# Attention and a gated MLP on one core: chunks 0 and 1 walk the weight tiles together, each unit's v comes in one transfer, and six attention units form the prologue

## The chip, the cores and the metric

The kernel runs on one core of one Trainium2 chip. The time is the device time of one execution in microseconds. The core's engines run side by side, each through its own instructions in a fixed order: TensorE (PE in the rows; its weight loads are PEld), VectorE (DVE), ScalarE (ACT), GpSimd (POOL) and SyncE (SP), whose queue issues all the transfers here.

## The reference

The first part is attention over 4 batches of 8 heads, 576 positions and 64 columns. Its output is the sum of a coarse attention over means of four positions, repeated four times, and a local one over the positions closer than 4. The second part is a two-layer MLP with 512 inputs, 2048 inner columns and 512 outputs.

```
q_d = q.reshape(B, H, Sd, 4, D).mean(axis=3)            # k_d, v_d alike
out_up = np.repeat(sm_attn(q_d, k_d, v_d), 4, axis=2)
mask = np.abs(pos[:, None] - pos[None, :]) < 4
out_local = softmax(np.where(mask, scale * q @ k.T, -1e9)) @ v
x = (out_up + out_local).transpose(0, 2, 1, 3).reshape(B * S, H * D)   # 2304 x 512
h = x @ w_in                                            # 2304 x 2048
g = h * np.tanh(np.log1p(np.exp(h)))
out = g @ w_out                                         # 2304 x 512
```

All of it is float32; the two weight matrices come as float64.

## The kernel before

**Attention units.** `attention(b, p, ...)` makes one unit: batch b and one pair of heads p, so 16 units of 576 columns. A unit loads its q and k (`qk`) and its v; VectorE pools q and k (L345); TensorE makes the coarse scores (`sc`, L360) and the local ones (`sl`, L390); softmax follows on VectorE and ScalarE (L363 to L405); TensorE transposes (`at`, `pt`) and multiplies with v (`pvo`, `pve`, L441 and L467); VectorE adds the two parts (L480) and splits the result into a high and a low part (L494). That is `x{p}_{c}`, in the layout that the MLP reads: x of p holds 128 of the 512 inputs, c is a chunk of 384 of the 2304 rows. A batch has 576 rows, so chunk 0 needs the four units of batch 0, and chunk 1 needs those of batches 0 and 1. v comes in three transfers: `vw`, windows of 48 positions on two groups of 48 partitions for the local part, and `vc` on 72 partitions, from which GpSimd (L415, L417) makes the pooled `vd`.

**Weights.** `load_w(f)` brings the tile of 128 inner columns f of `w_in` (`wi`) and `w_out` (`wo`) as 64-bit words into a `stg` buffer, of which there are three, and turns them into a high and a low float32 part: per half two ScalarE (L526, L535) and four VectorE instructions (L527, L529, L532, L536). There are 16 f tiles. They stay on the chip.

**Slots.** `slot(s, c, f, ...)` is one chunk with one f tile; there are 96. Twelve h matmuls (L553: four groups of three, one group for each p) fill one of two h buffers in PSUM. The gate follows: ScalarE L567, VectorE L568, ScalarE L570, L571, L573, VectorE L574, ScalarE L577, VectorE L579, which gives `g`. Then come nine acc matmuls (L590: three groups of three), which add to the chunk's three acc banks in PSUM. `SEGS` sets the walk: chunk 0 with f 0 to 4, chunk 1 with f 0 to 7, chunk 0 with f 5 to 15, chunk 1 with f 8 to 15, then chunks 2 to 5 one after the other. Where a segment ends early, ScalarE copies its three acc banks to SBUF (`parts`, L599), and the last segment of the chunk adds them (L605).

**The order.** Nothing is put in order by hand. `Plan.op` records each step with an estimated duration, its reads and writes and a priority; `Plan.order` places the steps, and each engine then runs what stands in its list, in that order. The priority of a step of slot s is about s, of its acc matmuls s + LAG - 0.5 (`LAG`: for s below 20, below 60 and above), of f tile f `WPRI[0] + WPRI[1] * f` (plus `WPRI[2]` for wo), of a unit `ATT` and `UNIT`, and of its v transfers `VOFF` more. The first `NPRO` units are the prologue: they use `SETS` buffer sets of their own beside the common set `att`, take them in turn, and share PSUM banks that the MLP's h and acc buffers take over only when the prologue is done. While TensorE has nothing to do, `fill` puts in matmuls on the identity (L686, `warm`, or into unused columns of an h bank).

Of the kernel before, what the change touches and what calls it, by code (L numbers as in the profile page):

```python
# [280 lines left out]
class Kernel:  # L281
    def __init__(self, tc, qk, vw, vc, w_in, w_out, out):
        self.tc, self.nc = tc, tc.nc
        self.qk, self.vw, self.vc = qk, vw, vc
# [256 lines left out]
    def slot(self, s, c, f, first, last, final):  # L541
        nc, pl = self.nc, self.plan
        op = pl.op
        h = pl.buf("moeps", "h", [P, 512], F32, 2, f"h{s}")
# [38 lines left out]
        if first:  # L583
            self.acc = [pl.buf("moeps", f"acc{i}", [P, 512], F32, 1, f"acc{s}_{i}") for i in range(3)]
        for i in range(3):
            a_ = self.acc[i]
# [16 lines left out]
            if (c, i) in self.part:  # L603
                part = self.part[c, i]
                op("dve", dve(512), lambda part=part, a_=a_, o=o: nc.vector.tensor_tensor(  # L605
                    out=o()[:, :512], in0=a_(), in1=part[0]()[:, c], op=ALU.add), r=[a_, part], w=[o], prio=s + 1)
            elif i % 2:
# [8 lines left out]
    def run(self, ctx):  # L616
# [44 lines left out]
        def slots(segs):  # L661
            nonlocal s
            for c, f0, f1, final in segs:
                for f in range(f0, f1):
                    self.slot(s, c, f, f == f0, f == f1 - 1, final)
                    s += 1
# [40 lines left out]
def _layout(np, q, k, v, moe_w_in, moe_w_out):  # L707
# [17 lines left out]
    return dict(qk=qk, vw=vw, vc=v2.reshape(B, H // 2, S // 8, 2, 4, 2 * D), w_in=w_in, w_out=w_out)  # L725
# [24 lines left out]
```

## Time and profile before

| | |
|---|---|
| median of 3 runs | 529.82 us (528.88 to 531.0) |
| profiled execution | 531.34 us |
| its span, first to last instruction | 529.3 us |
| mean granted TensorE clock | 0.990 |
| TensorE busy | 511.8 us (97%), 4997 matmuls |
| VectorE, ScalarE busy | 330.6 us (62%), 348.8 us (66%) |
| GpSimd busy | 39.0 us (7%) |
| moved by DMA | 43.60 MB, mean 82 GB/s |

Busy time is the time in which an engine executes; matmuls overlap one another, and so a busy TensorE need not be at its peak, and the filler matmuls count as busy too. The span lacks the 2 us around the first and the last instruction. The three runs lie 0.4% apart.

### The profile page before, as it was taken

How to read it: one execution, taken by the hardware profiler on the slowest of the kernel's cores; microseconds unless marked ns; L12 is line 12 of the kernel's file. 1: busy time of each engine (PE TensorE's matmuls, PEld its weight loads, DVE VectorE, ACT ScalarE, POOL GpSimd, SP SyncE). 2: the span in 40 equal slices, each digit the busy share in tenths (PEclk: the TensorE clock that was granted, in tenths of full speed). 3: DMA queues.
4: the chain of work that ended last, by engine and by line, in shares of the span. 5: the costliest groups of instructions: out<-in, count | busy, mean ns of one | idle time of the engine just before them, and what ended most of it. 6: DMA issues, size and time to landing. Idle time of an engine off the chain costs nothing.

```text
span 529.3 us, 11973 instructions
## 1 busy us (share of the span) xinstructions
PE 511.8 (97%) x4997; PEld 444.8 (84%) x4997; DVE 330.6 (62%) x696; ACT 348.8 (66%) x793; POOL 39.0 (7%) x53
## 2 busy tenths in 40 slices
PE   6799989999999999999999999999999999999997
PEld 4676778989999988887887888888898898989885
DVE  5599999999999353588887756524334243343333
ACT  3265867999988757475666667665656656566573
POOL 4421110000000000031211100000000000000000
PEclk9798999999999999999999999999999999999999
DMA  8764765434453010254444211100001000010001
GB/s 240 179 196 125 200 174 164 139 130 153 124 176 98 2 59 1 77 165 119 126 129 127 59 47 41 56 0 1 1 0 61 1 1 0 1 60 1 0 1 60
DMA packets 12950, 43.60 MB, mean 82 GB/s; under 512 B 1760, under 2 KB 1760, under 8 KB 12896
## 3 DMA queue, kind: packets, MB, share of 16 engines
q1 hardware_dynamic: 12896, 42.83, 27.0%
q8 instruction: 39, 0.64, 0.5%
q14 instruction: 15, 0.12, 0.1%
HBM read 38.11 MB, written 4.72 MB: 81 GB/s over the span
## 4 chain that ended last, share of the span: by engine, by line
PE 71%; DVE 6%; ACT 1%; issue 0%; DVEq 0%; ACTq 0%
PE acc L590 33%; PE h L553 32%; PE pve L467 1%; DVE x L494 1%; PE at L428 1%; PE pvo L441 1%; PE pvo L467 1%; PE sc L360 1%; PE pt L452 1%; DVE x L480 1%; PE sl L390 1%; DVE cst L365 1%; DVE cst L363 1%; DVE L_att L399 0%; DVE lst L398 0%; DVE mH L574 0%
## 5 line engine op out<-in xcount | busy, mean ns | idle before, releaser
L553 PE MATMUL h<-x,wi 128*128 128x384 f32 x1152 | 220.8, 340 | 0.7 <-DVE mH L574 0.5
L590 PE MATMUL acc<-wo,g 128*128 128x512 f32 x864 | 216.8, 396 | 0.5 <-DVE g L579 0.5
L553 PEld LDWEIGHTS h<-x,wi 128*128 128x128 f32 x1152 | 200.9, 188 | 11.4 <-DVE mH L574 3.0
L590 PEld LDWEIGHTS acc<-wo,g 128*128 128x128 f32 x864 | 160.0, 188 | 31.5 <-DVE g L579 0.9
L579 DVE SCALAR_TENSOR_TENSOR g<-mH,g 128x384 fp32r<-128x384 f32 (+1 forms) x98 | 55.5, 568 | 65.0 <-ACT g L577 64.9
L568 DVE TENSOR_SCALAR mA<-mA 128x384 f32<-128x384 f32 (+1 forms) x98 | 35.8, 366 | 89.7 <-ACT mA L567 89.5
L567 ACT ACTIVATE mA<-h 128x384 f32<-128x384 f32 (+1 forms) x98 | 47.0, 482 | 51.1 <-PE h L553 50.1
L570 ACT ACTIVATE mA<-mA 128x384 f32<-128x384 f32 (+1 forms) x98 | 50.6, 517 | 25.2 <-DVE mA L568 24.4
L577 ACT ACTIVATE g<-mH 128x384 fp32r<-128x384 f32 (+1 forms) x98 | 50.2, 515 | 22.6 <-PE acc L590 22.0
L571 ACT ACTIVATE mA<-mA,one 128x384 f32<-128x384 f32 (+1 forms) x98 | 59.3, 606 | 2.0
L574 DVE SCALAR_TENSOR_TENSOR mH<-mA,h 128x384 f32<-128x384 f32 (+1 forms) x98 | 52.9, 543 | 7.2 <-ACT mA L573 5.0
L573 ACT ACTIVATE mA<-mA 128x384 f32<-128x384 f32 (+1 forms) x98 | 50.2, 513 | 1.7
L415 POOL TENSOR_TENSOR vc<-vc 72x512 f32<-72x512 f32 x16 | 21.9, 1370 | 208.2 <-DVE cst L365 148.9
L367 ACT ACTIVATE A<-sc,cst 128x144 f32<-128x144 f32 x48 | 17.8, 375 | 17.2 <-DVE cst L365 16.9
L492 ACT ACTIVATE x<-x 128x384 fp32r<-128x384 f32 (+1 forms) x32 | 12.5, 437 | 20.6 <-DVE x L480 20.6
L345 DVE TENSOR_REDUCE qkd<-qk 128x288 f32<-128x1152 f32 x16 | 21.5, 1345 | 5.3 <-DMA qk<-in_qk_dram 5.2
L467 PEld LDWEIGHTS pve<-PT,vw 38*64 38x64 f32 x640 | 20.6, 135 | 3.7 <-ACT PT L459 3.1
L467 PE MATMUL pve<-PT,vw 38*64 38x32 f32 x640 | 22.4, 220 | 0.4 <-ACT PT L459 0.3
L686 PEld LDWEIGHTS <-ident 128*128 128x128 bf16 x173 | 15.4, 111 | 7.4 <-issue 2.4
L433 ACT ACTIVATE AT<-at 72x288 f32<-72x288 f32 x32 | 11.6, 400 | 13.8 <-PE at L428 13.8
L390 PEld LDWEIGHTS sl<-qk 64*32 64x32 f32 x1152 | 12.5, 111 | 9.8 <-issue 8.8
L390 PE MATMUL sl<-qk 64*32 64x38 f32 x1152 | 14.6, 202 | 5.3 <-issue 5.3
(75 smaller groups left out, 457.1 us busy)
## 6 DMA issues: line engine op xcount, KB each, us to landing
qk<-in_qk_dram SPq DMA_DIRECT2D x16, 582.0 KB, 8.6
...
vc<-in_vc_dram SPq DMA_DIRECT2D x16, 288.0 KB
...
vw<-in_vw_dram SPq DMA_DIRECT2D x16, 240.0 KB, 9.5
vw<-in_vw_dram SPq DMA_DIRECT2D x16, 192.0 KB, 4.3
```

The source lines that it names most:

```text
L390: nc.tensor.matmul(sl3()[64 * h + 32 * f:64 * h + 32 * f + 32, t], qk()[r_, 0, k0 + 3:k0 + 35], qk()[r_, 1, k0:k0 + KW], start=not pmask, ...
L467: nc.tensor.matmul(o_()[64 * h:64 * h + 64, c0:c0 + 32], vw()[64 * e:64 * e + KW, t // 2, f, 64 * h:64 * h + 64], PT()[64 * e:64 * e + KW, ...
L553: nc.tensor.matmul(h()[:, :CH], w()[:, a, kt * P:(kt + 1) * P], x()[:, b_, :], start=kt == 0 and j == 0, stop=kt == 3 and j == 2)
L567: op("act", act(n, True), lambda o_=o_: nc.scalar.activation(A()[:, o_], h()[:, o_], AF.Exp), r=[h_], w=[a_])
L568: op("dve", dve(n, True), lambda o_=o_: nc.vector.tensor_scalar(A()[:, o_], A()[:, o_], float(math.exp(20.0)), 1.0, op0=ALU.min, op1=ALU.a ...
L570: op("act", act(n), lambda o_=o_: nc.scalar.activation(A()[:, o_], A()[:, o_], AF.Square), w=[a_])
L571: op("act", act(n, False, 1), lambda o_=o_: nc.scalar.activation(A()[:, o_], A()[:, o_], AF.Ln, bias=self.one), w=[a_])
L573: op("act", act(n), lambda o_=o_: nc.scalar.activation(A()[:, o_], A()[:, o_], AF.Exp, scale=-1.0), w=[a_])
L574: op("dve", dve(n), lambda o_=o_: nc.vector.scalar_tensor_tensor(out=H()[:, o_], in0=A()[:, o_], scalar=0.5, in1=h()[:, o_], op0=ALU.subtr ...
L577: op("act", act(n), lambda o_=o_: nc.scalar.activation(g()[:, 0, o_], H()[:, o_], AF.Copy, scale=-2.0), r=[x_], w=[one])
L579: op("dve", dve(n), lambda o_=o_: nc.vector.scalar_tensor_tensor(out=g()[:, 1, o_], in0=H()[:, o_], scalar=-2.0, in1=g()[:, 0, o_].bitcast ...
L590: nc.tensor.matmul(a_(), g()[:, a, i * P:(i + 1) * P], wo()[:, b_], start=first and j == 0, stop=last and j == 2)
```

## The change

Chunks 0 and 1 now walk the f tiles together: after chunk 0 with f 0 and f 1 comes chunk 1 with f 0, then chunk 0 with f 2, chunk 1 with f 1, and so on to f 15 (`LEAD = 1`). Chunk 1 gets three acc banks of its own, the three that the units use later, so nothing is set aside in `parts` and nothing is added. All of a unit's v comes as one tile `vv`, 9216 bytes on each of 128 partitions, of which the first ten places hold the windows and the last eight the part for `vd`. The prologue has six units and three buffer sets of its own. The table of priorities and the estimated durations are new. The arithmetic of a unit, a weight tile and a slot stays. Further down in the file lines move: L410 is the v transfer, L492 what was L494, L525 to L534 what was L527 to L536, L552 and L591 the h and acc matmuls, L567 to L578 what was L568 to L579.

```diff
-LAG = (4.0, 6.5, 5.5)
+LAG = (2.5, 5.5, 5.5)
 FA = 5
-SETS = 2
-ATT = {0: (-900, 20), 1: (-46, 10.0), 2: (-25, 9.0), 3: (21, 13.5)}
-WPRI = (9.1, 0.8, 7.7)
-UNIT = {(0, 0): -1, (0, 1): -5, (0, 2): -2, (0, 3): -3, (1, 0): 5, (1, 1): 1, (1, 3): 1, (2, 0): 0, (2, 1): -1, (2, 2): 5, (2, 3): 2, (3, 0): 4, (3, 1): -1, (3, 2): 3, (3, 3): -2}
+SETS = 3
+ATT = {0: (-900, 20), 1: (-46, 10.0), 2: (5, 13.0), 3: (34, 5.5)}
+WPRI = (9.1, 0.67, 7.7)
+UNIT = {(0, 0): -3, (0, 1): -5, (0, 2): -2, (0, 3): -3, (1, 0): 5, (1, 1): -1, (1, 3): 1, (2, 0): -2, (2, 1): -1, (2, 2): 5, (2, 3): 2, (3, 0): 4, (3, 1): 2, (3, 2): 3, (3, 3): -2, (1, 2): -2}
 WARM = True
-NPRO = 4
+NPRO = 6
 STICK = 15
-VOFF = 40
-WDMA = 10
+VOFF = 10
+WDMA = 0
 PIPE0 = (2, 1, 0)
 PIPE1 = (1, 0, 1)
-SEGS = ((0, 0, 5), (1, 0, 8), (0, 5, 16), (1, 8, 16))
+LEAD = 1
 PMASK = (0, 1)
 NMISH = (3, 2)
 TAIL = 0
...
-        vw = buf("vw", [112, 5, 2, P])
         pv_ = pl.prio + VOFF
-        for i in range(2):
-            op("sp", 48 * (5 - i) * 1024 / RATE, lambda i=i: nc.sync.dma_start(
-                vw()[64 * i:64 * i + 48, :5 - i], self.vw[b, p, i, :, :5 - i]), w=[(vw, i)], prio=pv_)
-        vc, vd = buf("vc", [72, 2, 4, P]), buf("vd", [72, 2, P])
-        op("sp", 72 * 4096 / RATE, lambda: nc.sync.dma_start(vc(), self.vc[b, p]), w=[vc], prio=pv_)
+        vv, vd = buf("vv", [P, 18, P]), buf("vd", [72, 2, P])
+        op("sp", P * 18 * 512 / RATE, lambda: nc.sync.dma_start(vv(), self.vv[b, p]), w=[vv], prio=pv_)
+        vw = lambda: vv()[:, :10].rearrange("p (t f) c -> p t f c", f=2)
+        vc = lambda: vv()[:72, 10:].rearrange("p (c r) d -> p c r d", r=4)
...
         if first:
-            self.acc = [pl.buf("moeps", f"acc{i}", [P, 512], F32, 1, f"acc{s}_{i}") for i in range(3)]
+            where, tag = ("attps", "att1") if c == 1 else ("moeps", None)
+            self.acc[c] = [pl.buf(where, tag or f"acc{i}", [P, 512], F32, self.nb[where, tag] if tag else 1, f"acc{s}_{i}")
+                           for i in range(3)]
...
-            if not final:
-                part = self.part[c, i] = (self.parts[i], c)
-                op("act", act(512, True), lambda part=part, a_=a_, c=c: nc.scalar.activation(part[0]()[:, c], a_(), AF.Copy),
-                   r=[a_], w=[part], prio=s + 1)
-                continue
...
-        segs = [(c, f0, f1, f1 == self.NF) for c, f0, f1 in SEGS] + [(c, 0, self.NF, True) for c in range(max(SEGS)[0] + 1, 6)]
+        both = sorted([(f, 0, f) for f in range(self.NF)] + [(f + LEAD + 0.5, 1, f) for f in range(self.NF)])
+        todo = [(c, f) for _, c, f in both] + [(c, f) for c in range(2, 6) for f in range(self.NF)]
```

What the new priorities do to the order shows at three places. Names in these rows are those of the program: `x3_1` is x of p 3 and chunk 1, `h5` the h of slot 5, `acc5_0` bank 0 of the accumulation that slot 5 opens, `g8` the gate of slot 8, and the last number only tells buffers apart.

The first place is VectorE up to the last x of chunk 1. Before, these rows are the last of 181:

```order
L527 TENSOR_SCALAR tmp_wo4_1652<-stg_wo4_1509 128x512
L529 SCALAR_TENSOR_TENSOR stg_wo4_1509<-stg_wo4_1509,tmp_wo4_1652 128x512
L574 SCALAR_TENSOR_TENSOR mH3_1672<-mA3_1594,h3_1374 128x384
L532 SCALAR_TENSOR_TENSOR stg_wo4_1509<-stg_wo4_1509 128x512
L579 SCALAR_TENSOR_TENSOR g3_1679<-mH3_1672,g3_1679 128x384
L536 TENSOR_TENSOR wo4_1718<-stg_wo4_1509,wo4_1718 128x512
L480 TENSOR_TENSOR x32_1_3_1725<-pve1_3_1665,xd1_3_1661 128x5x64
L480 TENSOR_TENSOR x32_1_3_1725<-pvo1_3_1647,xd1_3_1661 128x4x64
L527 TENSOR_SCALAR tmp_wi5_1739<-stg_wi5_1645 128x512
L568 TENSOR_SCALAR mA4_1731<-mA4_1731 128x384
L494 TENSOR_TENSOR x3_1_886<-x32_1_3_1725,x3_1_886 128x192
```

After the change, these are the last of 150, and the next five:

```order
L478 TENSOR_TENSOR x32_1_3_1516<-pve1_3_1457,xd1_3_1453 128x5x64
L478 TENSOR_TENSOR x32_1_3_1516<-pvo1_3_1440,xd1_3_1453 128x4x64
L527 SCALAR_TENSOR_TENSOR stg_wi2_1384<-stg_wi2_1384,tmp_wi2_1510 128x512
L573 SCALAR_TENSOR_TENSOR mH1_1534<-mA1_1446,h1_1360 128x384
L492 TENSOR_TENSOR x3_1_937<-x32_1_3_1516,x3_1_937 128x192
L492 TENSOR_TENSOR x3_2_1532<-x32_1_3_1516,x3_2_1532 128x384
L530 SCALAR_TENSOR_TENSOR stg_wi2_1384<-stg_wi2_1384 128x512
L578 SCALAR_TENSOR_TENSOR g1_1543<-mH1_1534,g1_1543 128x384
L534 TENSOR_TENSOR wo1_1518<-stg_wo1_1184,wo1_1518 128x512
L534 TENSOR_TENSOR wi2_1554<-stg_wi2_1384,wi2_1554 128x512
```

The x of chunk 1 comes when two slots are under way, where there were five, and f tile 2 is converted behind it, where f tile 5 was.

The second place is where TensorE takes up the acc matmuls of a slot, here those of slot 8 before:

```order
L553 MATMUL h10_1958<-x2_1_785,wi5_1774 128x384 x3
L553 MATMUL h10_1958<-x3_1_886,wi5_1774 128x384 x3
L590 MATMUL acc5_1_1857<-wo2_1368,g7_1912 128x512 x3
L590 MATMUL acc5_2_1869<-wo2_1368,g7_1912 128x512 x3
L553 MATMUL h11_1993<-x0_1_517,wi6_1847 128x384 x3
L553 MATMUL h11_1993<-x1_1_606,wi6_1847 128x384 x3
L553 MATMUL h11_1993<-x2_1_785,wi6_1847 128x384 x3
L553 MATMUL h11_1993<-x3_1_886,wi6_1847 128x384 x3
L590 MATMUL acc5_0_1850<-wo3_1575,g8_1955 128x512 x3
```

and those of slot 7 after the change:

```order
L552 MATMUL h8_1804<-x0_1_430,wi3_1648 128x384 x3
L552 MATMUL h8_1804<-x1_1_622,wi3_1648 128x384 x3
L552 MATMUL h8_1804<-x2_1_772,wi3_1648 128x384 x3
L552 MATMUL h8_1804<-x3_1_937,wi3_1648 128x384 x3
L591 MATMUL acc2_0_1633<-wo2_1601,g6_1809 128x512 x3
L591 MATMUL acc2_1_1652<-wo2_1601,g6_1809 128x512 x3
L591 MATMUL acc2_2_1661<-wo2_1601,g6_1809 128x512 x3
L552 MATMUL h9_1853<-x0_0_428,wi5_1795 128x384 x3
L591 MATMUL acc0_0_1512<-wo4_1748,g7_1843 128x512 x3
L552 MATMUL h9_1853<-x1_0_619,wi5_1795 128x384 x3
```

The first acc group of slot 8 stood behind all four h groups of slot 11; that of slot 7 now stands behind the first h group of slot 9. For other slots below 20 it is the first or the second group, at times the fourth.

The third place is SP's queue of transfers, where f tile 3 is issued. Before:

```order
L524 DMA stg_wo2_1053<-in_w_out_dram 128x1024
L344 DMA qk1_2_1114<-in_qk_dram 128x1164
L524 DMA stg_wi3_1182<-in_w_in_dram 128x1024
L414 DMA vc1_3_1216<-in_vc_dram 72x1024
L524 DMA stg_wo3_1274<-in_w_out_dram 128x1024
L411 DMA vw1_2_1277<-in_vw_dram 48x1280
L411 DMA vw1_2_1277<-in_vw_dram 48x1024
L344 DMA qk1_3_1341<-in_qk_dram 128x1164
```

After the change:

```order
L410 DMA vv1_3_1291<-in_vv_dram 128x2304
L344 DMA qk2_0_1353<-in_qk_dram 128x1164
L522 DMA stg_wi2_1384<-in_w_in_dram 128x1024
L522 DMA stg_wo2_1413<-in_w_out_dram 128x1024
L410 DMA vv2_0_1520<-in_vv_dram 128x2304
L522 DMA stg_wi3_1575<-in_w_in_dram 128x1024
L522 DMA stg_wo3_1583<-in_w_out_dram 128x1024
```

The weights of f tile 3 stood ahead of the v of units (1,2) and (1,3). Now the v of unit (2,0) stands ahead of them, whose buffer is that of unit (1,3).

## Rows read from the trace of the kernel before

**Rows 1.** The page's part 1: busy us, share of the span, instructions.
```profile
PE 511.8 (97%) x4997; PEld 444.8 (84%) x4997; DVE 330.6 (62%) x696; ACT 348.8 (66%) x793; POOL 39.0 (7%) x53
```

**Rows 2.** Stretches to 96 us: length, busy us (instructions) by engine, clock, DMA.
```profile
core 0: us, PE busy (x) PEld busy (x) DVE busy (x) ACT busy (x) POOL busy (x), PEclk, DMA share, GB/s
0.00:10.00 10.00, 8.08 (x186) 5.90 (x186) 4.42 (x7) 1.79 (x4) 4.78 (x21) 1.00 0.85 258
10.00:20.00 10.00, 4.73 (x92) 3.42 (x89) 9.26 (x21) 2.81 (x12) 4.37 (x4) 0.71 0.97 211
20.00:40.00 20.00, 19.27 (x426) 15.60 (x425) 14.25 (x35) 11.73 (x37) 6.42 (x6) 0.97 0.62 177
45.00:50.00 5.00, 4.90 (x28) 3.56 (x27) 5.00 (x14) 0.81 (x3) 0.12 (x1) 0.66 0.31 109
40.00:96.00 56.00, 52.02 (x984) 43.33 (x984) 54.66 (x122) 39.55 (x105) 6.64 (x6) 0.97 0.57 166
```

**Rows 3.** Timeline around chunk 1's last x: start us, us, engine, line, operation.
```profile
95.27 0.35 DVE L494 TENSOR_TENSOR x<-x,x 128x192 fp32r<-128x192 f32 x1
...
95.54 0.69 DVE L529 SCALAR_TENSOR_TENSOR stg_wi<-stg_wi,tmp_wi 128x512 int32<-128x512 int32 x1
...
96.53 0.69 PE L553 MATMUL h<-x,wi 128*128 128x384 f32 x3
```

**Rows 4.** The chain that ended last, two pieces: start us, us, what.
```profile
435.39 0.70 PE acc L590 x3
436.09 2.11 PE h L553 x12
```

**Rows 5.** VectorE's groups by line, 96 to 173 us: busy us, mean ns, idle before.
```profile
L574 DVE SCALAR_TENSOR_TENSOR mH<-mA,h 128x384 f32<-128x384 f32 x19 | 10.4, 548 | 0.4 <-ACT mA L573 0.3
L579 DVE SCALAR_TENSOR_TENSOR g<-mH,g 128x384 fp32r<-128x384 f32 x18 | 9.9, 552 | 1.5 <-ACT g L577 1.5
L529 DVE SCALAR_TENSOR_TENSOR stg_wi<-stg_wi,tmp_wi 128x512 int32<-128x512 int32 x11 | 7.6, 688 | 0.1
...
L536 DVE TENSOR_TENSOR wi<-stg_wi,wi 128x512 fp32r<-128x512 f32 x11 | 7.5, 685 | 1.4 <-ACT wi L535 1.4
...
L568 DVE TENSOR_SCALAR mA<-mA 128x384 f32<-128x384 f32 x19 | 6.7, 352 | 0.1
L527 DVE TENSOR_SCALAR tmp_wo<-stg_wo 128x512 int32<-128x512 int32 x11 | 4.6, 421 | 0.2 <-ACT stg_wo L526 0.2
```

**Rows 6.** Timeline of the prologue: first landing, fillers, VectorE's waits, fifth L345.
```profile
4.58 2.77 DVE L345 TENSOR_REDUCE qkd<-qk 128x288 f32<-128x1152 f32 x2 [4.58 <-DMA qk<-in_qk_dram]
...
16.92 3.59 PE L686 MATMUL warm<-ident 128*128 128x256 bf16 x16
...
24.54 0.61 DVE L363 TENSOR_REDUCE cst<-sc 128x3 f32<-128x432 f32 x1 [4.56 <-PE sc L360]
...
34.34 1.34 DVE L345 TENSOR_REDUCE qkd<-qk 128x288 f32<-128x1152 f32 x1
```

**Rows 7.** The page's part 6, transfers of a unit: KB each, us to landing.
```profile
qk<-in_qk_dram SPq DMA_DIRECT2D x16, 582.0 KB, 8.6
...
vc<-in_vc_dram SPq DMA_DIRECT2D x16, 288.0 KB
...
vw<-in_vw_dram SPq DMA_DIRECT2D x16, 240.0 KB, 9.5
vw<-in_vw_dram SPq DMA_DIRECT2D x16, 192.0 KB, 4.3
```

**Rows 8.** Two later stretches, columns as in rows 2.
```profile
100.00:140.00 40.00, 39.91 (x202) 35.99 (x201) 36.75 (x74) 37.39 (x76) 0.00 (x0) 1.00 0.45 147
220.00:320.00 100.00, 98.26 (x1465) 82.06 (x1464) 78.21 (x163) 61.22 (x168) 16.81 (x16) 1.00 0.39 112
```

**Rows 9.** Timeline of slots 8 and 18: their h, and their L579.
```profile
106.84 2.24 PE L553 MATMUL h<-x,wi 128*128 128x384 f32 x12
...
114.78 0.54 DVE L579 SCALAR_TENSOR_TENSOR g<-mH,g 128x384 fp32r<-128x384 f32 x1
...
147.06 2.26 PE L553 MATMUL h<-x,wi 128*128 128x384 f32 x12
...
157.16 0.55 DVE L579 SCALAR_TENSOR_TENSOR g<-mH,g 128x384 fp32r<-128x384 f32 x1
```

More of the change, by code (lines that the diff above doesn't have):

```diff
@@ L281, with __init__ @@
 class Kernel:
-    def __init__(self, tc, qk, vw, vc, w_in, w_out, out):
+    def __init__(self, tc, qk, vv, w_in, w_out, out):
         self.tc, self.nc = tc, tc.nc
-        self.qk, self.vw, self.vc = qk, vw, vc
+        self.qk, self.vv = qk, vv
         self.w_in, self.w_out, self.out = w_in, w_out, out
@@ L360, in cmm @@
                     nc.tensor.matmul(pc3()[r_, m], qkd()[r_, 48 * m:48 * m + 64], qkd()[r_, C:], start=True, stop=True)
-        op("pe", 745, cmm, r=[qkd], w=[pc], cols=1728, gap=60)
+        op("pe", 845, cmm, r=[qkd], w=[pc], cols=1728, gap=60)
         op("dve", dve(3 * C) - 4, lambda: nc.vector.tensor_reduce(out=cst()[:, 0], in_=pc3(), op=ALU.max, axis=AX.X),
@@ L442, in xmm @@
                                      AT[kc]()[:, :, h, :], start=kc == 0, stop=kc == 1)
-        op("pe", 562, xmm, r=[vd, *AT], w=[pvo], cols=1296, gap=90)
+        op("pe", 650, xmm, r=[vd, *AT], w=[pvo], cols=1296, gap=90)
         xd = buf("xd", [P, C])
@@ L470, in pvmm @@
                                          start=True, stop=True)
-        op("pe", 1100, pvmm, r=[vw, PT], w=[pve, pvo], cold=2200, cols=1200, gap=75)
+        op("pe", 1230, pvmm, r=[(vv, 0), PT], w=[pve, pvo], cold=2200, cols=1200, gap=75)
         x32 = pl.buf(sb, "x32", [P, S], F32, 1, f"x32_{n}")
@@ L538, in load_w, with slot @@
             self.w[nm, f] = w
-    def slot(self, s, c, f, first, last, final):
+    def slot(self, s, c, f):
         nc, pl = self.nc, self.plan
         op = pl.op
+        first, last = f == 0, f == self.NF - 1
         h = pl.buf("moeps", "h", [P, 512], F32, 2, f"h{s}")
@@ L596, in slot @@
                 continue
-            if not final:
-                part = self.part[c, i] = (self.parts[i], c)
-                op("act", act(512, True), lambda part=part, a_=a_, c=c: nc.scalar.activation(part[0]()[:, c], a_(), AF.Copy),
-                   r=[a_], w=[part], prio=s + 1)
-                continue
-            o = pl.buf("stg", "stg", [P, 1024], F32, self.nstg, f"o{c}_{i}")
[L603 to L607, printed above, removed]
+            o = pl.buf("stg", "stg", [P, 1024], F32, self.nstg, f"o{c}_{i}")
+            if i % 2:
                 op("dve", dve(512), lambda a_=a_, o=o: nc.vector.tensor_copy(o()[:, :512], a_()),
@@ L637, in run @@
         self.plan = pl = Plan(pool)
-        self.nstg, self.part = 3, {}
+        self.nstg, self.acc = 3, {}
         self.nb = {("attps", "att1"): 3, ("props", "att1"): 4}
@@ L657, in run, with slots @@
             self.load_w(f)
-        segs = [(c, f0, f1, f1 == self.NF) for c, f0, f1 in SEGS] + [(c, 0, self.NF, True) for c in range(max(SEGS)[0] + 1, 6)]
+        both = sorted([(f, 0, f) for f in range(self.NF)] + [(f + LEAD + 0.5, 1, f) for f in range(self.NF)])
+        todo = [(c, f) for _, c, f in both] + [(c, f) for c in range(2, 6) for f in range(self.NF)]
         s = 0
-        def slots(segs):
+        def slots(todo):
             nonlocal s
[L663 to L666, printed above, removed]
+            for c, f in todo:
+                self.slot(s, c, f)
+                s += 1
         def units(bs):
@@ L673, in run @@
         units((1,))
-        k = len(SEGS)
-        self.parts = [pl.buf("att", t, [P, 2, 512], F32, 1, f"parts_{t}") for t in ("qk", "vw", "vc")]
-        slots(segs[:k])
+        slots(todo[:32])
         units((2, 3))
-        slots(segs[k:])
+        slots(todo[32:])
         done = pl.gate = pl.op("pe", 0, lambda: None, after=gate, prio=-1000)
@@ L699, in tile_kernel @@
 @with_exitstack
-def tile_kernel(ctx: ExitStack, tc, qk, vw, vc, w_in, w_out, out):
-    Kernel(tc, qk, vw, vc, w_in, w_out, out).run(ctx)
+def tile_kernel(ctx: ExitStack, tc, qk, vv, w_in, w_out, out):
+    Kernel(tc, qk, vv, w_in, w_out, out).run(ctx)
 _OUTS = [((2304, 512), "float32")]
@@ L724, in _layout @@
     w_in = w_in.reshape(M // P, P, F // P, P).transpose(2, 1, 0, 3).reshape(F // P, P, M)
[L725 removed]
+    return dict(qk=qk, vv=vv, w_in=w_in, w_out=w_out)
 def kernel(**inputs):
```

17 lines of the change are left out of this document (9 added, 8 removed).

## The prediction

> **What bounds the kernel now.** I read the page's busy shares first: TensorE is busy 97% of the span [rows 1]. So TensorE's work sets the time, and a change can gain only where TensorE does something other than its 1152 h and 864 acc matmuls and the attention. The stretches say where that is [rows 2, 8]. From 100 to 140 us TensorE is busy 39.91 of 40 us, while from 40 to 96 VectorE is the full engine: 54.66 of 56 us, and TensorE has gaps. Busy TensorE time there hides filler matmuls (L686) and short attention matmuls, so I looked for the moment at which its queue becomes dense. The timeline has it: VectorE writes the last piece of chunk 1's x (L494, 128x192) from 95.27 to 95.62, and the matmul group that reads it starts at 96.53 [rows 3]. Slot 5 is the first that needs batch 1. Behind that group the chain of work is h x12 and acc x9 without a gap, 2.11 us and 3 x 0.70 us a slot [rows 4]. So the kernel has two parts: a VectorE-bound one until about 96 us, and a TensorE-bound one whose length is the work then left.
>
> **The change, part by part.** I make the sum against the profiled execution (span 529.3, its own time 531.34 us; the median of the runs is 529.82, so 1.5 less), and carry the difference over to the median.
>
> *VectorE ahead of chunk 1's last x.* In the old order 180 instructions stand ahead of that L494, in the new one 149. Fewer are 6 of L527, 5 of L529, 6 of L532, which does the same amount of work, 7 of L536 (weights of five f tiles before, not quite two now) and of the slots 3 of L568, 2 of L574, 3 of L579. By their means [rows 5] that is 6 x 0.42 + 5 x 0.69 + 6 x 0.69 + 7 x 0.685 + 3 x 0.35 + 2 x 0.55 + 3 x 0.55 = 18.7 us. Consecutive ones overlap: in [rows 3] the L529 at 95.54 starts 0.08 before the L494 ends, so I take 0.08 off each of the 32: 16.1. One pooling reduce (L345, of unit (2,0)) is added, 1.34 less 0.08. Net 14.9 us less, nothing hidden, since VectorE is full there.
>
> *VectorE's idle time ahead of it.* The longest stretch is 4.56 us before 24.54, a wait for sc of the third unit [rows 6]. TensorE was not short of time for that sc: it ran 16 filler matmuls in 3.59 us ahead of the at matmuls, with a granted clock of 0.71 over 10 to 20 us [rows 2, 6]. With a fourth buffer set and six units in the loose prologue the order gives VectorE other units' work there. I take 4.6 us back. The bounds: at most 9 (idle in 0 to 40 us are 5.6 + 0.7 + 5.8 by [rows 2], less the 4.58 before the first landing [rows 6], and 1.3 more to 96 us), at least -2 if the transfers come late, which is next.
>
> *One v transfer of 128 x 9216 bytes.* It moves 1152 KB where 240 + 192 + 288 went [rows 7]. In the new order qk and v of four units go first, then qk of unit (1,0): 5 x 582 + 4 x 1152 = 7518 KB, 7.7 MB. The old stretch from 10 to 20 us, with its transfers to 48 and 72 partitions, moved 211 GB/s at a share of 0.97, so 218 GB/s when full; that from 100 to 140, with 128-row weight transfers, 147 at 0.45, so 327 [rows 2, 8]. Add 2.7 us for issue and latency: unit (1,0)'s qk lands at 38 us by the slow row, at 26 by the fast one. VectorE wants it at about 30 (its L345 starts at 34.34 in the old trace [rows 6], with nearly the same work ahead; less 4.6). The new shape is nearest to the fast row, so I take no wait; the slow row is the -2 above. [...] The 7 MB more in all cost nothing later: the DMA share is 0.45 in 100 to 140 us.
>
> So chunk 1's last x comes 14.9 + 4.6 = 19.5 us earlier, at about 76 us.
>
> *What TensorE then still has to do.* In the old order 69 h matmuls and 30 acc matmuls stand ahead of the group that waits for that x, in the new one 33 and 9. So 12 h groups of three and 7 acc groups of three are left over: 12 x 2.11 / 4 + 7 x 0.70 = 11.2 us [rows 4]. The earlier start is paid for largely by work that the old order had already done while it waited.
>
> *The wait behind it.* Slot 3 needs f tile 2, whose L534 stands five places behind the x on VectorE: by [rows 5], less overlap, 0.47 + 0.60 + 0.47 + 0.60 + 0.60 = 2.7 us plus a signal. TensorE has one h group (0.53) and one acc group (0.70) for it: it idles 1.8 us.
>
> *LAG from 4.0 to 2.5 in the first 20 slots.* Old: a slot's acc stands behind all of the h of the third slot after it. New: it stands behind the first or second h group of the slot after next, 6 x 0.70 + 5.5 x 0.53 = 7.1 us behind the end of its own h. The chain between, five ScalarE and three VectorE instructions, took 6.2 us for slot 8 (h ends at 109.08, its L579 at 115.32) and 8.4 for slot 18 (149.32, 157.71) [rows 9]. No row has this distance; the bounds are 0, and 1.3 us on each of 17 slots, 22 us. I take 3. The value is nearer to the first, since a late g delays the h matmuls too and so eases the load that made it late: VectorE needs 2 x (4 weight instructions, 2.2 us, + 3 slot instructions, 1.2 us) = 6.8 us for the two slots that cost TensorE 8.4, where the old order had it 92% busy from 100 to 140 us [rows 8].
>
> *Nothing* for the dropped parts copies (6 of L599) and adds (6 of L605, which become copies): TensorE stays full around them (39.91 of 40 us in 100 to 140). *Nothing* for attention in the second half: the same eight units interleave with other spacing; TensorE was idle 1.7 us in all from 220 to 320 [rows 8], so at most that is gained, and I allow as much the other way.
>
> Sum: -19.5 + 11.2 + 1.8 + 3.0 = -3.5. Span 525.8; on the median 529.82 - 3.5, **526.3 us**.
>
> **The rivals.** (a) *More comes back*: VectorE waits only for the first landing (-9) and no acc is late (0): -14.9 - 9 + 11.2 + 1.8 = -10.9, 519 us. For it speaks the fourth set; against it that weights no longer fill VectorE's gaps between 40 and 60 us. (b) *No change*: the gain is moved, not made. VectorE has the same conversions and units to do until the last weight; if its idle time only moves from 20 us to 50, the 4.6 is lost, and -14.9 + 11.2 + 1.8 + 3 = +1.1, 531 us. [...] (d) *Slower*: the short lag. The acc matmuls wait for g in each of 17 slots, and TensorE executes in order, so the h groups behind wait too. It decides from (3.5 + 3.0 + 2.65) / 17 = 0.54 us a slot, that is a chain of 7.6 us on average, between the two of [rows 9]. At 0.8 us it gives -6.5 + 13.6 = +7.1, 537 us.
>
> **How the numbers follow.** Forecast, with its own range of 522.5 to 528.5, 0.42; (a) 0.18; (b) 0.17; (c) 0.10; (d) 0.13. A measurement of this kernel can tell about 0.5%, 2.65 us. Below 527.2 lie (a) and most of the forecast: 0.58. Within it lie (b), (c) and the forecast's upper edge: 0.29; above 532.5, (d): 0.13. The range leaves out the best of (a) and most of (d): 518.5 to 532.
>
> **What the changed profile would show.** The L492 row of 128x192 that ends batch 1 at 72 to 81 us, TensorE dense two or three us later; the first h matmul near 60 us, since h's banks come free when the sixth unit is done, not the fourth; VectorE idle less than 9 us in 0 to 40; TensorE's waits for g (L578) in 80 to 150 us below 5 us in total; a DMA share in the first 25 us above 0.8 at over 260 GB/s. It is wrong if x comes after 83 us; if TensorE has gaps ahead of most acc groups; or if the weight transfer of f tile 3, which now stands behind unit (2,0)'s v in SP's queue and so waits for the last unit's buffer, holds slot 5 up: each us of that is added in full.

## The result and the profile after

The changed kernel takes 535.65 us (median of 14 runs), the one before 530.84 beside it: a ratio of 1.0092, interval 1.0065 to 1.0118. It is slower by 0.9%, where 526.3 us was forecast. The profiled execution has a span of 531.8 us and takes 533.54 itself, 2.2 more than the profiled one of before. The other runs lie between 531.5 us at a mean granted clock of 0.994 and 539.7 at 0.980, and the ratios leave out the few runs that, as the last one, stand far above the rest.

The first row is the page's part 1. The stretches behind it answer to [rows 2] and end at chunk 1's last x.

```profile
PE 510.0 (96%) x4962; PEld 442.0 (83%) x4962; DVE 328.6 (62%) x692; ACT 349.8 (66%) x791; POOL 39.0 (7%) x54
```

```profile
core 0: us, PE busy (x) PEld busy (x) DVE busy (x) ACT busy (x) POOL busy (x), PEclk, DMA share, GB/s
0.00:10.00 10.00, 7.41 (x119) 5.40 (x119) 4.56 (x9) 2.78 (x8) 6.99 (x24) 1.00 0.83 327
10.00:20.00 10.00, 7.93 (x262) 6.37 (x262) 9.10 (x19) 5.08 (x18) 3.97 (x4) 1.00 1.01 413
20.00:30.00 10.00, 9.61 (x223) 7.73 (x218) 9.11 (x25) 4.64 (x17) 4.00 (x4) 1.00 0.79 294
30.00:40.00 10.00, 6.48 (x173) 5.17 (x172) 5.47 (x14) 3.37 (x13) 2.06 (x2) 0.77 0.40 154
35.00:40.00 5.00, 3.44 (x37) 2.94 (x39) 1.24 (x3) 1.30 (x4) 1.08 (x2) 0.54 0.03 6
40.00:82.50 42.50, 36.99 (x811) 29.58 (x808) 38.49 (x89) 26.93 (x81) 4.25 (x4) 0.97 0.45 154
```

In the trace of before, the two stretches in the middle read:

```profile
20.00:30.00 10.00, 9.81 (x219) 7.82 (x218) 4.93 (x12) 5.30 (x18) 3.91 (x4) 0.95 0.50 140
30.00:40.00 10.00, 9.46 (x215) 7.78 (x209) 9.33 (x24) 6.43 (x21) 2.51 (x2) 1.00 0.73 213
```

Up to 30 us VectorE and the transfers go as forecast: VectorE is idle for 7.2 us, where it was 11.4, and from 10 to 20 us 413 GB/s move where there were 211. Then VectorE, the engine that sets this part, is busy 5.47 of 10 us, and from 35 to 40 only 1.24 of 5. The timeline around chunk 1's last x answers to [rows 3]:

```profile
82.06 1.55 PE L591 MATMUL acc<-wo,g 128*128 128x512 f32 x6
82.14 0.82 DVE L492 TENSOR_TENSOR x<-x,x 128x192 fp32r<-128x192 f32 x2
...
82.88 0.68 DVE L530 SCALAR_TENSOR_TENSOR stg_wi<-stg_wi 128x512 int32<-128x512 int32 x1
...
83.45 0.69 PE L552 MATMUL h<-x,wi 128*128 128x384 f32 x3
```

The 128x192 piece starts at 82.14 and takes 0.35, so x is there at 82.49: 13.1 us earlier than before, not 19.5. From there to the end of the span it is 449.3 us, against 529.3 - 95.62 = 433.7 before: 15.6 more, where the forecast had 11.2 + 1.8 + 3.0 = 16.0. So the part behind x came out at nearly the forecast length, and the miss of the profiled execution lies ahead of it.

What VectorE waits for there, on its own timeline:

```profile
33.64 0.60 DVE L373 TENSOR_TENSOR A<-A,cst 128x432 f32<-128x432 f32 x1
37.66 0.49 DVE L478 TENSOR_TENSOR x<-pve,xd 128x320 f32<-128x320 f32 x1 [3.42 <-PE pve L465]
...
40.56 0.61 DVE L363 TENSOR_REDUCE cst<-sc 128x3 f32<-128x432 f32 x1 [1.67 <-PE sc L360]
```

And TensorE, in the middle of the group of pv matmuls that VectorE waits for:

```profile
32.76 0.28 PE L465 MATMUL pve<-PT,vv 38*64 38x32 f32 x2
36.56 0.32 PE L465 MATMUL pve<-PT,vv 38*64 38x32 f32 x2 [3.52 <-issue]
```

"Issue" means that the engine waited for nothing that the profile shows, no operand, bank or weight. TensorE's waits of that kind up to 90 us, by line (us in total, times, longest), in the changed kernel:

```profile
PE sl L390 <- issue: 3.7, 3, 1.8
PE pve L465 <- issue: 3.5, 1, 3.5
PE at L426 <- issue: 1.9, 1, 1.9
```

What is late, as the run with one transfer held shows below, is TensorE's own program. It comes by DMA, as the kind "instruction" among the queues: q8 moves 39 packets of 16 KB in the whole execution, for some 10,000 TensorE instructions. From 30.4 to 34.1 us the queues moved data, but for one packet of 8 KB on q14; the next block on q8 comes in the 1.1 us behind (queue, kind: packets, MB, share of 16 engines; the two stretches apart):

```profile
q1 hardware_dynamic: 227, 1.32, 89.9%
q14 instruction: 1, 0.01, 0.5%
...
q1 hardware_dynamic: 24, 0.06, 15.6%
q8 instruction: 1, 0.02, 5.4%
```

In the trace that block lands at 35.12, and TensorE goes on at 36.56. Counted in all its instructions in the trace (matmuls, weight loads and a few that wait for semaphores), the gaps put down to "issue" (here from start to start) stand behind instruction 705 (1.7 us), 961 (0.6), 1473 (3.7), 2241 (2.0) and 2497 (2.2), and the 5.47 us gap of before behind 449: all of them multiples of 256 apart, and each ended 1.3 to 1.4 us after a q8 packet had landed. So a packet goes with a block of 256 instructions (9,999 of them and 39 packets in this trace), and up to 80 us each packet starts after the block before its own has begun: there the trace shows one block ahead and no more. At 32.8 us that was not enough: the small matmuls of attention used the block before up in 2.4 us (30.45 to 32.82) while 1152 and 512 KB of data, issued at 27.52 and 27.90, were under way, and the next packet started only at 34.16.

The old trace has the same gap at another place:

```profile
10.33 0.54 PE L390 MATMUL sl<-qk 64*32 64x38 f32 x36
16.14 0.85 PE L390 MATMUL sl<-qk 64*32 64x38 f32 x36 [5.27 <-issue]
```

### The profile page after: what moved, and what is told of

Its sections match the earlier page's. It is cut to its first block, busy times and chain, and to the rows that moved or that the text cites. A ratio compares the mean times of both kernels' runs of the same rounds, so it can differ in the third digit from the quotient of the medians.

```text
span 531.8 us, 11848 instructions
## 1 busy us (share of the span) xinstructions
PE 510.0 (96%) x4962; PEld 442.0 (83%) x4962; DVE 328.6 (62%) x692; ACT 349.8 (66%) x791; POOL 39.0 (7%) x54
## 4 chain that ended last, share of the span: by engine, by line
PE 62%; DVE 3%; issue 1%; POOL 0%; ACT 0%; DVEq 0%
PE h L552 28%; PE acc L591 27%; PE pve L465 1%; PE sl L390 1%; PE sc L360 1%; PE pvo L439 1%; PE pt L450 1%; PE pvo L465 1%; PE at L426 1%; DVE g L578 0%; DVE mH L573 0%; DVE A L373 0%; DVE lst L403 0%; POOL vv L413 0%; POOL vd L415 0%
## 5 line engine op out<-in xcount | busy, mean ns | idle before, releaser
L552 PE MATMUL h<-x,wi 128*128 128x384 f32 x1152 | 226.3, 340 | 2.4 <-DVE mH L573 1.9
L591 PE MATMUL acc<-wo,g 128*128 128x512 f32 x864 | 220.3, 395 | 0.1
L552 PEld LDWEIGHTS h<-x,wi 128*128 128x128 f32 x1152 | 201.3, 188 | 17.7 <-DVE mH L573 8.1
L591 PEld LDWEIGHTS acc<-wo,g 128*128 128x128 f32 x864 | 160.1, 188 | 29.1 <-DVE g L578 1.1
L567 DVE TENSOR_SCALAR mA<-mA 128x384 f32<-128x384 f32 (+1 forms) x98 | 34.7, 355 | 93.3 <-ACT mA L566 93.2
L578 DVE SCALAR_TENSOR_TENSOR g<-mH,g 128x384 fp32r<-128x384 f32 (+1 forms) x98 | 54.0, 553 | 57.2 <-ACT g L576 57.2
L413 POOL TENSOR_TENSOR vv<-vv 72x512 f32<-72x512 f32 x16 | 20.9, 1306 | 294.6 <-PE at L426 172.5
L465 PEld LDWEIGHTS pve<-PT,vv 38*64 38x64 f32 x640 | 20.8, 136 | 7.0 <-issue 4.5
L465 PE MATMUL pve<-PT,vv 38*64 38x32 f32 x640 | 22.8, 222 | 3.6 <-issue 3.5
L345 DVE TENSOR_REDUCE qkd<-qk 128x288 f32<-128x1152 f32 x16 | 21.5, 1345 | 4.8 <-DMA qk<-in_qk_dram 4.8
L431 ACT ACTIVATE AT<-at 72x288 f32<-72x288 f32 x32 | 11.8, 401 | 14.1 <-PE at L426 14.1
L478 DVE TENSOR_TENSOR x<-pve,xd 128x320 f32<-128x320 f32 x16 | 7.8, 490 | 17.3 <-PE pve L465 16.8
L465 PE MATMUL pvo<-PT,vv 38*64 38x32 f32 x512 | 18.4, 222 | 0.0
```

What stands on the lines that cost most here:

```text
L465: nc.tensor.matmul(o_()[64 * h:64 * h + 64, c0:c0 + 32], vw()[64 * e:64 * e + KW, t // 2, f, 64 * h:64 * h + 64], PT()[64 * e:64 * e + KW, ...
L552: nc.tensor.matmul(h()[:, :CH], w()[:, a, kt * P:(kt + 1) * P], x()[:, b_, :], start=kt == 0 and j == 0, stop=kt == 3 and j == 2)
L567: op("dve", dve(n, True), lambda o_=o_: nc.vector.tensor_scalar(A()[:, o_], A()[:, o_], float(math.exp(20.0)), 1.0, op0=ALU.min, op1=ALU.a ...
L578: op("dve", dve(n), lambda o_=o_: nc.vector.scalar_tensor_tensor(out=g()[:, 1, o_], in0=H()[:, o_], scalar=-2.0, in1=g()[:, 0, o_].bitcast ...
L591: nc.tensor.matmul(a_(), g()[:, a, i * P:(i + 1) * P], wo()[:, b_], start=first and j == 0, stop=last and j == 2)
```

## The experiments

Ratios are to the kernel before, run beside each. The runs stand in groups of one chip, and the median of before was 530.02 beside those from "three v transfers" to "old walk", 529.09 beside those from "one transfer held" to "old places", 530.31 beside the first run with three held and "v held", and 530.58 beside the other two; across groups, ratios compare and medians do not. "x" is the end of chunk 1's last x in the run's profile, "issue" the sum of TensorE's issue waits up to 100 us there.

| kernel | median us | ratio, interval | x, us | issue, us |
|---|---|---|---|---|
| before | 530.84 | | 95.6 | 6.3 |
| changed | 535.65 | 1.0092 (1.0065 to 1.0118) | 82.5 | 9.1 |
| changed, three v transfers | 541.45 | 1.0199 (1.0163 to 1.0236) | 89.8 | 11.8 |
| changed, old lags | 535.16 | 1.0081 (1.0046 to 1.0115) | 86.7 | 8.6 |
| before, new walk | 547.03 | 1.0330 (1.0287 to 1.0372) | 97.3 | 5.2 |
| changed, old walk | 541.09 | 1.0213 (1.0168 to 1.0257) | 86.9 | 7.9 |
| changed, one transfer held | 530.54 | 1.0046 (1.0006 to 1.0086) | 83.5 | 7.2 |
| before, one v transfer | 537.71 | 1.0145 (1.0106 to 1.0183) | 99.8 | 4.2 |
| changed, more fillers | 536.13 | 1.0120 (1.0076 to 1.0163) | 82.1 | 4.9 |
| changed, old places of batches 2, 3 | 536.14 | 1.0105 (1.0064 to 1.0146) | 81.1 | 7.2 |
| changed, three held | 528.72 | 0.9986 (0.9956 to 1.0016) | 74.8 | 3.3 |
| the same again | 528.27 | 0.9960 (0.9934 to 0.9986) | 75.3 | 3.4 |
| three held, three v transfers from batch 2 on | 529.68 | 0.9991 (0.9964 to 1.0019) | 77.1 | 5.0 |
| before, v held | 532.45 | 1.0027 (0.9989 to 1.0066) | 94.7 | 0.8 |

**Three v transfers in the changed kernel**, issued at the same places:

```diff
-        op("sp", ..., lambda: nc.sync.dma_start(vv(), self.vv[b, p]), w=[vv], prio=pv_)
+        def load_v():
+            for i in range(2):
+                nc.sync.dma_start(vw()[64 * i:64 * i + 48, :5 - i], self.vw[b, p, i, :, :5 - i])
+            nc.sync.dma_start(vc(), self.vc[b, p])
+        op("sp", ..., load_v, w=[vv], prio=pv_)
```

> The changed kernel with each unit's v again in three transfers (240, 192 and 288 KB in place of 1152 KB), issued at the same places of SyncE's queue; all other engines keep the changed kernel's order instruction for instruction. Theory 1 (TensorE waits for its own instructions: in the changed kernel's trace it stands still for 3.74 us at 32.8 in the middle of a pv group, with no wait on a semaphore, until an instruction block has landed at 35.12, while 1152 and 512 KB of data are under way): 38% fewer bytes make the blocks earlier, the gap at that place is under 2 us, chunk 1's last x comes at 78 to 81 us in place of 82.5, and the time is 531 to 534 us. Rival 1 (bytes don't matter, the units' own chain sets the pace): x at 82 to 83, 535 to 536.5 us. Rival 2 (transfers on 48 and 72 partitions are slow, as the old trace's 218 GB/s had it): unit (1,0)'s qk lands after 30 us in place of 22.8 and the time is 537 us or more.

It took 541.45 us, and rival 2 fits: the first stretches of its profile show a DMA share as high as the changed kernel's at 220 to 255 GB/s, and TensorE has a gap of 4.3 us from 19.8 to 24.0, for a block that lands at 22.4 (columns as above). The qk of unit (1,0) landed at 29.2 in place of 22.8, a little ahead of the rival's 30. Theory 1's "fewer bytes, earlier blocks" fell: in these rows fewer bytes are under way for longer.

```profile
0.00:10.00 10.00, 7.21 (x117) 5.31 (x118) 3.82 (x6) 1.80 (x3) 6.34 (x24) 1.00 0.85 220
10.00:20.00 10.00, 8.02 (x235) 6.14 (x232) 9.41 (x21) 6.01 (x22) 2.63 (x3) 1.00 1.02 223
20.00:30.00 10.00, 5.98 (x66) 4.50 (x66) 3.96 (x9) 0.95 (x4) 3.85 (x4) 0.66 0.94 255
```

**Old lags in the changed kernel** (`LAG = (4.0, 6.5, 5.5)`).

> The changed kernel with the old lags between h and acc, 4.0, 6.5, 5.5 in place of 2.5, 5.5, 5.5. Theory 1 (instruction blocks in the prologue; the lag costs about 1 us, since the changed trace shows 0.1 us lost per 10 us from 110 on): 534 to 536.5 us. Rival (the short lag is what made it slower, forecast rival d): 531 us or less, with TensorE denser between 83 and 120 us.

535.16, as theory 1 had it: by the medians the lag is worth 0.5 us, which the intervals cannot tell from nothing. (x lay at 86.7 in a profile whose clock fell at 63 us; its mean is 0.978, in the changed kernel's 0.992.)

**The walk alone in the kernel before, and the old walk in the changed kernel.**

```diff
-        segs = [(c, f0, f1, f1 == self.NF) for c, f0, f1 in SEGS] + ...
+        both = sorted([(f, 0, f) for f in range(self.NF)] + [(f + LEAD + 0.5, 1, f) for f in range(self.NF)])
+        todo = [(c, f) for _, c, f in both] + [(c, f) for c in range(2, 6) for f in range(self.NF)]
```

> The kernel before with the walk of the change alone: chunks 0 and 1 share each f tile, acc of chunk 1 in the banks of the attention, no parts copies; prologue, lags and transfers as before. Theory 1 and the forecast's own term agree that slots done while VectorE is waited for are lost: chunk 1's last x some 8 to 12 us earlier (weights of three f tiles less ahead of it), 11 to 14 us of left-over TensorE work behind it: 531 to 536 us. Rival (the walk is the whole loss, the prologue a pure gain): 538 us or more. Rival (the walk is a pure gain): 529 us or less.

> The changed kernel with the old walk: chunk 0 f 0-4, chunk 1 f 0-7, chunk 0 f 5-15, chunk 1 f 8-15, with parts copies; six units in the prologue, one v transfer and the short lag stay. Theory 1 (the prologue is what loses, by late instruction blocks and the slow clock behind them): chunk 1's last x at 88 to 94 us in place of the 95.62 of before, 530 to 534 us. Rival (the prologue gains, the walk loses): 528 us or less. Rival (the prologue loses much more with this walk, since h cannot start before the sixth unit is done): 536 us or more.

Both were slower than expected, 547.03 and 541.09, so neither part is the whole loss and they don't add: the new walk costs 3.3% with the old prologue and saves 1.2% with the new one. In the first the old table of priorities still puts 180 VectorE instructions ahead of x, x comes no earlier (97.3), and TensorE has 45 h and 18 acc matmuls done by then, where before it had 69 and 27. In the second x comes 8.7 us earlier, and the part behind it is 454.4 us long, 20.7 more than before; where the rest over the left-over work went was not followed up.

**One transfer held.** VectorE writes one column of the v buffer of unit (1,1) behind the L373 of 33.64, so the transfer into it, and wi of f tile 0 behind it on SyncE, start about 6.9 us later. Nothing else moves in any engine's order.

```diff
+        clear.fn = lambda: nc.vector.memset(vv()[:, 0, :1], 0.0)
+        order.insert(order.index(self.mark["A", 0, 3]) + 1, clear)
```

> The changed kernel with one instruction more: VectorE writes one column of the v buffer of unit (1,1) (which the transfer then overwrites) right behind the row that scales A of unit (0,3), at 34.24 us in the changed trace. So that v transfer of 1152 KB (issued at 27.52 there), and the 512 KB of f tile 0 behind it in SyncE's queue, start at about 33 to 34 us, and nothing is under way from 30.5 to then. All else has the changed kernel's order. Theory 1 (TensorE's instruction block is late because of data under way): the block that landed at 35.12 lands by 32.5, the gap of 3.74 us at 32.82 is under 1 us, chunk 1's last x comes 2 to 4 us earlier (78.5 to 80.5), 531.5 to 533.5 us. Rival (blocks are late for another reason, the data under way has nothing to do with it): a gap of over 3 us at the same place, the time within 1 us of 535.65 or, if the late v or weights are missed later, above.

A ratio of 1.0046, where the changed kernel had 1.0092: about half of the loss, though the two intervals overlap. (The run with the old places below, whose transfers up to x are the changed kernel's, took 536.1 on the same chip.) The instruction block of 35.12 now lands at 32.47, alone on the queues from 30.4 to 34.1:

```profile
q8 instruction: 1, 0.02, 2.2%
```

and TensorE's gap at that place is 0.78 us, where it was 3.52:

```profile
33.87 0.25 PE L465 MATMUL pve<-PT,vv 38*64 38x32 f32 x2 [0.78 <-issue]
```

VectorE is busy 9.38 of the 10 us from 30 to 40, and x of p 3 and chunk 0 comes 4.5 us earlier (45.0, 49.5 in the changed kernel). In this profile it was lost again further on, and chunk 1's last x, at 83.5, missed the expected 78.5 to 80.5: another gap at the end of a block, 2.2 us to 57.3, and behind it the lower clock (columns as above, the last three are clock, DMA share and GB/s):

```profile
55.00:60.00 5.00, 2.83 (x16) 1.80 (x16) 3.22 (x8) 1.48 (x4) 0.00 (x0) 0.62 0.33 105
60.00:65.00 5.00, 4.94 (x56) 3.46 (x55) 1.98 (x3) 2.71 (x6) 0.00 (x0) 0.50 0.01 3
65.00:70.00 5.00, 5.00 (x113) 4.01 (x110) 3.44 (x8) 1.36 (x5) 0.00 (x0) 0.52 0.49 179
```

Eight of its twelve runs kept a mean clock of 0.993 or more and took 528.7 to 531.7 us; the profiled one is among the four at 0.980 to 0.989, which took 535.0 to 536.3.

**One v transfer in the kernel before** (`vv` in place of `vw` and `vc`, all numbers as before).

> The kernel before with all of a unit's v in one transfer of 1152 KB as the only change (the parts of chunk 0 and 1 lie in the buffers of qk and v). The run with three transfers in the changed kernel came out 5.8 us slower than the one with one. Theory 1: the transfers to 48 and 72 partitions hold the first units up, so one transfer brings the x of unit (0,0) and all behind it 3 to 6 us earlier and chunk 1's last x to 90 to 93 us; since TensorE still has the same slots to do while it waits, 525 to 528.5 us. Rival (the old prologue waits for TensorE's instruction block, 5.47 us at 10.67, which more bytes make later): 530 us or more.

537.71 lies in the rival's range, but not for the rival's reason: with more bytes the block landed at 11.2, not 14.74, and the gap of 5.47 us is 2.54. x of p 3 and chunk 0 came 6.3 us earlier (41.5), so the first units do gain; chunk 1's last x came 4.1 later (99.8), with issue gaps of 2.3 and 1.9 us and low clock from 63.9 to 70.7 (0.94 in the mean from 40 to 100). The transfer joined as one moved the planner's order too (TensorE has 78 h and 42 acc matmuls done by x), so this run does not part its causes.

**More fillers** (`PACE` 2.4 in place of 1.6).

> The changed kernel with the planner's pace for filler matmuls at 2.4 in place of 1.6: 153 fillers of 256 columns ahead of the MoE part in place of 102. If the slow clock behind TensorE's gaps (0.5 from 35.4 to 42.2 us in the changed trace) and its spread from run to run (mean clock 0.980 to 0.994, 531.5 to 539.7 us) is what costs: clock 0.992 or more in the runs, 531 to 533.5 us. Theory 1 (late instruction blocks; fillers are instructions too, 102 more of them): no gain, 535 to 539 us, with gaps of over 2 us at block ends as before.

536.13: no gain, though the clock was 0.989 to 0.997. The longest issue wait was 1.4 us here, not over 2 as expected, and VectorE's idle time ahead of x fell from 15.8 to 10.8 us; but x came at the same time (82.1), since the planner, with 56 fillers more to place, put 157 VectorE instructions ahead of it, where there were 149, and VectorE was busy for 71.3 us, not 66.7. Behind x TensorE was busy 17.06 of the 20 us from 80 to 100 at a clock of 0.91, in the changed kernel 19.46 at 1.00. So this run changed more than the clock, and what the clock alone is worth it does not show.

**Old places of the units of batches 2 and 3.**

```diff
-ATT = {..., 2: (5, 13.0), 3: (34, 5.5)}
+ATT = {..., 2: (-25, 9.0), 3: (21, 13.5)}
```

> The changed kernel with the old places of the eight units of batches 2 and 3 (the numbers of ATT and UNIT for them); the order up to chunk 1's last x stays. In the profiles attention took TensorE 38.5 us in the changed kernel and 34.0 in the one before (sum of its rows to the start of the next row, behind that x). If the new places cost that: 531 to 533.5 us. If they cost nothing or little (the rows between units differ in any case, since acc and sc durations in the plan differ): 534.5 to 536.5 us.

536.14: nothing came back, so the new places cost nothing that these runs can tell. The 4.5 us that the expectation names depend on how rows are cut: taken from the start of each matmul to the start of the next, attention behind x is 39.3 us in the changed kernel, 38.4 in this run and 36.7 in the one before.

**Three transfers held**: also v of unit (1,2) with wo of f tile 0, and qk of unit (1,3) with wi of f tile 1.

```diff
+HOLDS = ((("v", 1, 1), ("A", 0, 3), ...), (("v", 1, 2), ("lst", 1, 1), ...), (("qk", 1, 3), ("cst", 1, 2), ...))
```

> The changed kernel with three transfers held back in the way of the run with the one late v transfer (VectorE writes one column of the buffer that the transfer overwrites): v of unit (1,1) as there; v of unit (1,2) and with it wo of f tile 0, from 41.87 to about 45.3; qk of unit (1,3) and with it wi of f tile 1, from 50.30 to about 53. In the run with one held, TensorE still stood 1.87 us before 49.85 and 2.45 us before 57.34 at ends of instruction blocks, each with those transfers under way, and in its slower runs the granted clock fell to 0.5 at 56.2, right behind the second gap. Theory 1 (blocks late behind data): both gaps under 0.8 us, no low clock from 56 on in most runs, chunk 1's last x at 77 to 80, 525.5 to 529 us. Rival (the late blocks at these two places have another reason, or the slow clock comes anyway): gaps or clock as before, 529 to 532 us. Rival (data now come late for the units): 533 us or more.

> The run with three transfers held back, once more, beside the next kernel on one chip. 526 to 531 us, 0.995 to 1.002 of the kernel before; chunk 1's last x at 74 to 78 us in a run whose granted clock stays up to 70 us.

528.72, and 528.27 with the interval below 1; the first run's interval takes in 1. The two gaps that the expectation names, 1.87 and 2.45 us with one held, are 0.15 and 0.11 us in both profiles. Waits of TensorE and stretches in the second of the two:

```profile
PE sl L391 <- issue: 1.7, 2, 1.3
...
PE warm L678 <- issue: 0.9, 1, 0.9
PE pve L466 <- issue: 0.8, 1, 0.8
```

```profile
20.00:30.00 10.00, 9.61 (x219) 7.62 (x217) 9.31 (x23) 4.71 (x17) 4.00 (x4) 1.00 0.71 273
30.00:40.00 10.00, 8.37 (x270) 6.51 (x271) 9.37 (x26) 5.51 (x21) 0.00 (x0) 1.00 0.48 172
40.00:75.50 35.50, 32.57 (x712) 26.69 (x709) 34.24 (x80) 24.73 (x71) 6.57 (x6) 1.00 0.54 186
```

VectorE is busy 9.37 of 10 us from 30 to 40, where it was 5.47, and x comes at 75.3: the forecast's 76. The clock stays up to x in this profile. Its span is 526.2, 3.1 under before's, where the forecast was 3.5; the medians are 1.6 and 2.3 us under those of before beside them.

**Three v transfers from batch 2 on, with three held.**

> The kernel with three transfers held back, and the v of batches 2 and 3 again in three transfers (720 KB in place of 1152 KB), in the same order. In its trace TensorE stood 0.82 and 1.37 us at ends of instruction blocks (241 and 324 us) and 1.91 us at 304 us, where the v of unit (3,1) landed at 303.2, 7.4 us after its issue. If the bytes of the one transfer cost that behind 200 us: 1 to 3 us less than the kernel beside it. Rival (transfers on 48 and 72 partitions take as long for fewer bytes, as the run with three transfers in the changed kernel had it): the same within 1 us, or 1 to 3 us more.

529.68, 1.4 more than the kernel beside it, with intervals that overlap: the 1 to 3 us less did not come, and whether the three transfers are worse there is not shown.

**v held in the kernel before**, behind the second L345.

```diff
+HOLDS = ((("v", 0, 0, 0), ("qkd", 0, 1), ...),)
```

> The kernel before with one VectorE instruction more: it writes one column of the v buffer of unit (0,0) behind the second qkd reduce (7.35 us in the old trace), so that the v transfers of the first units, issued from 2.12 us on, start at about 7.4 us and the three qk transfers of the start are alone until then. In the old trace TensorE stood still from 10.67 to 16.14 us at the end of an instruction block that landed at 14.74. Theory 1 (blocks late behind data): the block lands by 11, the gap is under 1.5 us, chunk 1's last x comes 3 to 5 us earlier (91 to 93), 526 to 528.5 us. Rival (the data themselves are the limit up to 25 us, so the units wait for v and qk by as much): x within 1.5 us of 95.6 and 529 to 533 us.

The block came at 8.73 in place of 14.74, the gap of 5.3 us was gone, and VectorE's wait for the third unit's sc, 4.56 us in [rows 6], was a third of that:

```profile
19.52 0.61 DVE L364 TENSOR_REDUCE cst<-sc 128x3 f32<-128x432 f32 x1 [1.56 <-PE sc L361]
```

x of p 3 and chunk 0 came 3.6 us earlier; the time did not follow, 532.45. Between 64 and 86 us ScalarE waited 1.7 us for a transfer of wo, VectorE was busy 3.46 of 5 us from 70 to 75, the clock fell at 75.0 (0.66 from 75 to 80), and chunk 1's last x had 0.9 us left of the lead. A gap removed is worth what the next wait leaves of it.

## Why the prediction was wrong

**VectorE's work ahead of x** (-14.9): right. Its busy time to 82.5 us is 4.56 + 9.10 + 9.11 + 5.47 + 38.49 = 66.7; to 96 it was 82.6 in [rows 2], of which 0.4 lie behind x: 15.5 less.

**VectorE's idle time** (-4.6, bounds -9 to +2): the step that failed. To x it is 82.5 - 66.7 = 15.8 us, where it was 96 - 82.6 = 13.4: 2.4 more, not 4.6 less, so beyond its bound, and 7.0 us off. The prediction read the 4.56 us wait of [rows 6] as a matter of order, since TensorE ran 16 fillers ahead of the at matmuls. But those fillers stood behind a gap of 5.27 us in which TensorE had no instructions (the block landed at 14.74), and in the run with v held in the kernel before, where that gap is gone, 1.56 us of the wait are left. The new order did come by this gap: its TensorE reaches the end of that block at 14.2 us, not 10.7, and the next had landed at 11.4. So up to 30 us the gain is there, 7.2 us of idle time where it was 11.4. Then the same kind of gap came at 32.8 us, with the slower clock behind it (0.50 from 35.4 to 42.2): from 30 to 40 us VectorE is idle for 4.5 us (0.7 before), and from 40 to x for 4.0 (1.3 before). The sum had nothing for a wait of TensorE for its own instructions. The run with one transfer held shows the cause at 32.8 us, since it differs in when two transfers start; with three held the idle time is 75.5 - 66.5 = 9.0, that is 4.4 less than before, and the term is what was forecast.

**x at about 76**: 82.5, for that reason alone; 75.3 with three held.

**Left-over TensorE work** (+11.2): right. Ahead of the group that waits for x TensorE ran 33 h and 9 acc matmuls, before 69 and 30: 36 x 0.176 + 21 x 0.233 = 11.2.

**The wait for f tile 2 and the lag** (1.8 + 3.0): their sum is nearly right, the part behind x being 15.6 longer, not 16.0, but by luck. Both were sized too high: f tile 2 shows as fillers that take 0.6 us from 83.98 on, and for the lag TensorE waited 0.8 us for mH from 80 to 150 us and never for g. The other 3 us lie elsewhere: 1.4 in two issue waits at 248 and 329 us, the rest was not followed up.

**The transfer** (no wait): right for data, qk of unit (1,0) landed at 22.8, the share was 0.93 at 375 GB/s in the first 25 us. What it did to TensorE's instructions was not in the sum. Its 2.7 us for issue and latency is an estimate that the first landing of before bears out: 4.58 us in [rows 6], of which 582 KB take 1.8 at 327 GB/s. Why the rate goes with the shape no run shows. In the trace of before, one of the semaphores that count landings serves 4 vc transfers (72 rows) and 11 others and has 228 updates, 11 x 16 + 4 x 13, and the other seven come out in the same way; but the share from 10 to 20 us was 0.97 with the old transfers as well, at 211 GB/s, where it is 1.01 at 413.

**Sum**: -3.5 + 6.4 (x) - 0.4 (behind x) = +2.5, the spans' difference. The median is another 2.1 above the profiled execution, where before's is 0.5 below. These 2.6 us are open: the changed kernel's runs have mean clocks of 0.980 to 0.994, and which part of that hangs on the late blocks is not settled, though three held brought the mean clock to 0.99 or more in 23 of 24 runs, where it was 9 of 14.

**The rivals.** (a) did not come; even with three held 4.4 us of idle time came back, not 9. (b), idle time that only moves, was the right kind, from 20 us to 35, with 531 too small a price, since the wait grew on its way. (c), the slower clock in dense work: the clock did fall, to 0.50 from 35.4 to 42.2, but among the units, not in slots 2 to 4. In the trace of before it was 0.50 twice: from 14.27 to 21.09, within and behind the gap of 5.27 us, and from 44.99 to 48.40, behind a gap of only 0.77. That a gap brings it on is not shown. (d), the mechanism given for a slower time, did not happen. **The signs**: x at 82.5 missed its 72 to 81, VectorE's idle time in 0 to 40 us was 11.8, not below 9, and the first h came at 64.67, not near 60; the waits for g and the DMA share were as forecast. None of the signs of being wrong came: x is just short of 83, TensorE has no wait ahead of an acc group behind x, and the transfer of f tile 3 held nothing up (TensorE's waits from 80 to 150 us are the 0.8 for mH).
